# Reordering the loads and the preparation at the start of an attention and S4 convolution kernel

## The chip, the cores and the metric

The kernel runs on one core of one Trainium2 chip. The metric is the device time of one execution in microseconds (us). The engines: TensorE (PE, with its weight loads as PEld), VectorE (DVE), ScalarE (ACT), GpSimd (POOL), and SyncE (SP), which here only issues transfers; ACT and POOL issue some as well. SBUF is the on-chip memory, PSUM holds matmul results.

## What is computed

Two layers on separate inputs, each 2048 positions by 576 channels, whose outputs are put side by side:

```python
qkv = x @ wqkv                                # (2048,576) @ (576,1728), 32 heads of 18
scores = q k^T / sqrt(18), a key at most 255 positions back, softmax, @ v
a = that @ wo
# S4: one convolution kernel of 2048 taps for each channel
K[d,l] = Re sum_n C[d,n] * exp(dt[d]*A[d,n]*l) * dt[d]*B[d,n]        # n = 0..127, dt = exp(log_dt)
b = causal convolution of u with K (by FFT of length 4096) + u * Dskip
```

All inputs and outputs are float32, and the kernel keeps that accuracy with cheaper matmuls: an operand is scaled by a power of two and split into a high and a low float16 part (or into up to three bfloat16 parts).

## The kernel before

**Stages.** The program has a front (loads, scales, splits), then a loop up to about 423 us that runs three streams interleaved, then the transform of the convolution's taps, then the attention with the convolution beside it, and the output projection. Only the front and the way the loop begins are touched.

**The front of the projection** (`proj` up to its first yields, L184). To split x and wqkv it needs one power of two for each, from the largest magnitude of the whole array. `amax` (L163) takes the maximum of a block on DVE; `pow2_max` (L141) takes the maximum of those and reduces it over the 128 partitions on POOL; `pow2_of` (L149) turns it into the scale with four small DVE instructions. x is read for this as a flat block of 128 rows in four pieces and a rest, into the buffers that wh and wl will have later and into one of pool `pst`. Then wqkv comes in four column blocks of 432 by `load_rows` (L135), three transfers a block: rows 0 to 511 as four row groups of 128, and rows 512 to 575 twice, into both halves of the fifth group. So the fifth group holds its 64 rows doubled, and a matmul of 128 rows does their high and low parts in one. The weights' splits follow, per block wh on ACT (L215) and wl on DVE (L216).

**The front of the tables** (`s4_prep`, L274). It loads dt and A in two layouts, the multipliers c_ca, c_cm, c_cp and c_ct, and B and C, all from ACT's queue. It forms dt\*A (real and imaginary) over 96 partitions, three copies of 32, and `split3` (L261) splits each into three bfloat16 parts, one for each copy: `al` and `ps`, the stationary operands of the tables' matmuls (`outer`, L315). `wr` and `wi` are the products of B, C and dt.

**The loop's streams** are generators, and `merge` (L78) takes a step now of one and now of another, by the share that each has done. `proj`: for four chunks of 512 tokens, x comes in two halves, is split (L232 on ACT, L233 and L235 on DVE), and nine tiles of q and k and eight half tiles of v follow, 14 matmuls each (`mm14`, L166). A tile goes from PSUM by one ACT and one DVE instruction. Tiles and the u step share three PSUM buffers (pool `pps`). `tables`, for 36 groups of channels: exponents on ACT (mab, mg), phases by `fraction` (L324) on ACT and DVE, sines on ACT, `factors` on POOL (tr, t, A), `products` on POOL (m, L390), the Q table on DVE, and `taps` on PE (L428). `s1_u`: the first transform of u in 16 steps, 8 matmuls each.

**Order.** The order in which the program writes the instructions is not that of the engines in the front and the loop: a scheduler sets the order of each queue by its own estimates, with earlier written work first when several are ready. Inside `manual_schedule` the instructions keep the written order on each engine (the attention uses this already). In the profile before, instructions of that block stand on SP and DVE between ones written outside. Instructions on one engine run in the order of its queue, and one that waits holds those behind it.

## Time and profile before

| | |
|---|---|
| three runs | 1047.87, 1048.56, 1053.68 us; median 1048.56 |
| the profiled execution | 1042.13 us, span 1040.4 us, mean granted TensorE clock 0.968 |
| busy in the span | PE 81%, DVE 68%, ACT 55%, POOL 56% |
| moved from and to HBM | 88.60 MB read, 61.01 MB written |
| first projection matmul | 83.46 us |
| first product of the tables | 90.21 us |
| last tap | about 423 us |

Busy time of PE counts a matmul from its start to its modelled end, so a high share is not a peak rate. A group's line has the code line, engine, operation, output, inputs and shape; "idle before <-" names what ended the wait. In a table of stretches each engine's busy time is followed by its count of instructions.

### The profile page before, as it was taken

What the parts mean: (1) busy time and instruction counts of PE and PEld (TensorE: products, weight loads), DVE (VectorE), ACT (ScalarE), POOL (GpSimd) and SP (SyncE); (2) the same over time, 40 slices, a digit from 0 to 9 for tenths busy, and PEclk for the clock granted to TensorE, in tenths of its full rate; (3) what the DMA queues carried; (4) which work ended last, traced back from release to release, by engine and by line L of the source; (5) the groups of instructions that cost most, each with busy time, mean ns of one, the idle gap of its engine ahead of it and who ended that gap; (6) DMA issues with size and microseconds to landing.
All of it is one profiled execution on the core that took longest, in us unless ns stands there. A gap on an engine that the chain in (4) does not pass through costs nothing.

```text
span 1040.4 us, 26877 instructions
## 1 busy us (share of the span) xinstructions
PE 840.5 (81%) x10364; PEld 448.8 (43%) x10364; DVE 710.3 (68%) x1806; ACT 572.3 (55%) x895; POOL 585.5 (56%) x714
## 2 busy tenths in 40 slices
PE   0148997997989899677888888878887989988788
PEld 0024465565556457444343333323333444444345
DVE  2887567556565575655768888778877767678454
ACT  0486666665766666233565655645655555644461
POOL 0007768566576586200466676647775847766770
PEclk9998999999999899889899999989999999999999
DMA  9934444453543344564544465445634563579863
GB/s 272 286 93 119 99 111 120 111 127 88 128 110 91 75 95 92 158 198 128 160 125 143 136 184 176 116 124 160 202 104 143 169 183 99 141 193 240 232 180 124
DMA packets 151383, 151.74 MB, mean 146 GB/s; under 512 B 36808, under 2 KB 129224, under 8 KB 150552
## 3 DMA queue, kind: packets, MB, share of 16 engines
q1 hardware_dynamic: 143624, 131.45, 46.3%
q0 software_dynamic: 6128, 14.60, 5.1%
q10 hardware_dynamic: 1504, 3.99, 1.3%
q8 instruction: 81, 1.33, 0.6%
q14 instruction: 46, 0.38, 0.1%
HBM read 88.60 MB, written 61.01 MB: 144 GB/s over the span
## 4 chain that ended last, share of the span: by engine, by line
PE 41%; DVE 21%; DMA 13%; issue 9%; ACT 7%; POOL 4%; SPq 3%; DVEq 0%; ACTq 0%; POOLq 0%
PE pp L174 9%; PE r L648 5%; PE po L712 5%; PE r L918 4%; PE pp L472 3%; PE kp L428 3%; PE r L511 3%; PE r L519 3%; PE ST L689 3%; DVE jk L655 2%; PE x L320 2%; DMA c_ca<-in_c_ca_dram 2%; DVE qb L639 2%; DMA gk<-g 2%; DMA K<-in_wqkv_dram 2%
## 5 line engine op out<-in xcount | busy, mean ns | idle before, releaser
L655 DVE CUSTOM_DVE_ANT_0 jk<-r,bias 128x288 f32<-128x288 f32 (+7 forms) x512 | 199.8, 433 | 87.1 <-PE r L648 84.8
L700 POOL TENSOR_SCALAR_AFFINE_SELECT P<-P 128x512 f32<-128x512 f32 x240 | 167.7, 727 | 162.1 <-ACT P L691 159.6
L691 ACT ACTIVATE P<-ST,esc 128x1024 f32<-128x1024 f32 (+1 forms) x192 | 202.2, 1058 | 93.9 <-PE ST L689 93.3
L390 POOL TENSOR_TENSOR m<-A,tr 128x1024 f32<-128x1024 f32 x72 | 145.7, 2046 | 88.4 <-PE kp L428 88.4
L648 PE MATMUL r<-K,qb 128*64 128x288 f16 (+7 forms) x1024 | 130.1, 298 | 41.4 <-DVE t L542 11.5
L648 PEld LDWEIGHTS <-qb 128*64 128x64 f16 x1024 | 60.4, 110 | 124.5 <-issue 67.5
L712 PE MATMUL po<-P,V 128*32 128x256 f32 (+2 forms) x1408 | 100.6, 400 | 15.7 <-POOL P L700 6.1
L548 POOL TENSOR_TENSOR Y<-t,t 64x288 f32<-64x288 f32 x64 | 53.2, 831 | 75.9 <-DVE t L543 74.0
L472 PE MATMUL pp<-ut,w 128*128 128x288 f32 x128 | 44.3, 476 | 61.2 <-DMA ut<-in_u_dram 46.7
L428 PE MATMUL kp<-Q,m 128*32 128x64 f32 x4608 | 77.3, 220 | 7.8 <-issue 5.2
L428 PEld LDWEIGHTS kp<-Q,m 128*32 128x32 f32 x4608 | 67.8, 110 | 29.5 <-issue 23.3
L689 PE MATMUL ST<-Q,K 64*128 64x384 f16 (+2 forms) x704 | 74.0, 282 | 3.5 <-DMA Q<-mt 3.5
L130 ACT ACTIVATE g<-pp 128x288 f32<-128x288 f32 x96 | 36.9, 411 | 50.5 <-DMA gk<-g 24.9
L712 PEld LDWEIGHTS po<-P,V 128*32 128x32 f32 x1408 | 36.4, 111 | 50.3 <-issue 30.8
L472 PEld LDWEIGHTS pp<-ut,w 128*128 128x128 f32 x128 | 25.5, 215 | 74.1 <-issue 46.9
L549 POOL TENSOR_TENSOR Y<-t,t 64x288 f32<-64x288 f32 x64 | 53.9, 842 | 3.7
L174 PE MATMUL pp<-xh,wh 128*128 128x512 f16 x180 | 49.3, 392 | 6.8 <-DVE xh L235 5.2
L368 POOL TENSOR_TENSOR tr<-tr,mab 128x768 f32<-128x768 f32 x18 | 33.0, 1833 | 38.0 <-ACT tr L337 37.8
L331 DVE TENSOR_TENSOR k<-x,k 128x512 f32<-128x512 f32 (+1 forms) x54 | 34.0, 639 | 29.7 <-ACT k L330 29.2
L243 DVE SCALAR_TENSOR_TENSOR qst<-pp,qst 128x512 f16<-128x512 f32 x36 | 24.6, 684 | 42.8 <-ACT qst L242 29.1
L472 PE MATMUL pp<-K,w 128*128 128x288 f32 x128 | 44.0, 488 | 11.4 <-ACT g L130 10.0
L174 PEld LDWEIGHTS <-wh 128*128 128x128 f16 x324 | 31.8, 100 | 45.2 <-issue 11.9
(175 smaller groups left out, 1768.4 us busy)
## 6 DMA issues: line engine op xcount, KB each, us to landing
gx<-g SPq DMA_DIRECT2D x32, 288.0 KB
qd<-qst SPq DMA_DIRECT2D x72, 128.0 KB
gk<-g SPq DMA_DIRECT2D x32, 288.0 KB
tx<-gx SPq DMA_DIRECT2D x16, 576.0 KB
tk<-gk SPq DMA_DIRECT2D x16, 576.0 KB
h<-ho SPq DMA_DIRECT2D x16, 576.0 KB
Q<-qd SPq DMA_DIRECT2D x32, 216.0 KB
vd<-vst SPq DMA_DIRECT2D x16, 304.0 KB
```

The costliest lines, as they stand in the source:

```text
L174: self.nc.tensor.matmul(ps, u, v, start=(i == 0), stop=(i == len(ops) - 1))
L390: self.nc.gpsimd.tensor_tensor(m, A[:, ch, a0:a0 + 8].unsqueeze(3).to_broadcast(sh), tr[:, ch, part, 0:8].unsqueeze(2).to_broadcast(sh), o ...
L428: nc.tensor.matmul(kp[32 * st:32 * st + 32, c % 2 * JJ2 + j, :], m[:, ch, a0:a0 + 32], Q[:, ch, term % 2, :], start=(term == 0), stop=(ter ...
L472: nc.tensor.matmul(ps, self.w1[:, part, :], src[:, o:o + k], start=True, stop=True)
L548: nc.gpsimd.tensor_tensor(Y[par][0:64], t1[sl, 0], t2[sl, 0], op=OP.subtract)
L549: nc.gpsimd.tensor_tensor(Y[par][64:128], t1[sl, 1], t2[sl, 1], op=OP.add)
L648: nc.tensor.matmul(ps[64 * b:64 * b + 64, :n], self.qb[:, b, t, :], d["K"][:, b, k0:k0 + n], start=True, stop=True, skip_group_check=True)
L655: nc.vector.tensor_tensor_reduce(out=jk[:, :n], in0=ps[:, :n], in1=self.bias[:, 288 - n:], scale=1.0, scalar=-3e38, op0=OP.add, op1=OP.max ...
L689: nc.tensor.matmul(ps[:, u, o:o + n], d["K"][h, jp, k0:k0 + 128], d["Q"][h, jp, q0:q0 + n], start=True, stop=True, skip_group_check=True)
L691: nc.scalar.activation(pt[:, 2 * jp:2 * jp + 2, lo:hi], ps[:, :, lo:hi], AF.Exp, scale=self.esc)
L700: nc.gpsimd.affine_select(v, v, pattern=[[0, 4], [sg, 128]], compare_op=OP.is_ge, fill=0.0, base=-1 if far else 0, channel_multiplier=-sg)
L712: nc.tensor.matmul(self.po[32 * j:32 * j + 32, t0 * 128:t1 * 128], V[:, kb * 76 + 19 * j:kb * 76 + 19 * j + 32], pt[:, j, o:o + (t1 - t0) ...
```

## The change

The loads get a written order on SP: wqkv in four blocks, n_A_re, the first two halves of x (512 tokens), n_A_im, the other tokens of x as flat blocks in two buffers, dt, and the four parameters. The multipliers and one small input stay on ACT's queue. The host lays x and wqkv out so that a block is a single transfer with the doubled rows in it. The first two halves of x give part of the maximum and stay for the first split, so that these tokens are read once. Scales, splits and the tables' operands are written beside them in one function, `front`, whose order is fixed on each engine by `manual_schedule`. The three passes over ps (one product, two differences) move from DVE to POOL. The operand al gets its second and third parts from one residue in place; two ACT copies over 32 partitions each become one over 64. The weights' scale is formed ahead of that of x, by a reduction of its own. In the first merge stand one step for x, six projection tiles, 16 table steps and one u step, where four weight splits, 16 table steps and two u steps stood; the second merge has 49 projection steps in place of 56, and 15 u steps in place of 14. `load_rows`, `pow2_scale`, `split3` and `s4_prep` go.

```diff
+def columns(m, n):
+
+    r = m[np.r_[0:576, 512:576]].reshape(5, 128, -1, n)
+    return np.ascontiguousarray(r.transpose(1, 2, 0, 3))
+
+
...
+    def load_x(self, b):
+        t = self.p["raw"].tile([128, 5, 256], F32, name="raw")
+        self.nc.sync.dma_start(t, self.a["x"][:, b])
+        return t
+
+    def split_w(self, c, part):
+        cs = slice(c * 432, c * 432 + 432)
+        wh, wl = self.w
+        if part == 0:
+            self.nc.scalar.activation(wh[:, :, cs], self.wf[:, c], AF.Copy, scale=self.sw)
+        else:
+            self.nc.vector.scalar_tensor_tensor(wl[:, :, cs], self.wf[:, c], self.sw, wh[:, :, cs],
+                                                op0=OP.mult, op1=OP.subtract)
+
+    def split_x(self, raw):
+        nc = self.nc
+        xh = self.p["x"].tile([128, 5, 512], F16, name="xh")
+        xl = self.p["x"].tile([128, 4, 512], F16, name="xl")
+        for hf, t in enumerate(raw):
+            h = xh[:, :, hf * 256:hf * 256 + 256]
+            nc.scalar.activation(h, t, AF.Copy, scale=self.sx)
+            nc.vector.scalar_tensor_tensor(xl[:, :, hf * 256:hf * 256 + 256], t[:, 0:4], self.sx, h[:, 0:4],
+                                           op0=OP.mult, op1=OP.subtract)
+            nc.vector.scalar_tensor_tensor(h[64:128, 4], t[64:128, 4], self.sx[64:128], h[64:128, 4],
+                                           op0=OP.mult, op1=OP.subtract)
+        return xh, xl
+
+    def front(self):
+
+
+        nc, a, wp, sp, s4, tp = self.nc, self.a, self.p["wq"], self.p["const"], self.p["s4c"], self.p["prep"]
+        tt, pt, act = nc.vector.tensor_tensor, nc.gpsimd.tensor_tensor, nc.scalar.activation
+        self.mul, par, nA, flat = {}, {}, {}, []
+        dtn = tp.tile([96, NQ], F32, name="dtn")
+        dt = tp.tile([128, D], F32, name="dt")
+        for n in ("A_re", "A_im"):
+            nA[n] = tp.tile([96, NQ, 128], F32, name="n" + n)
+        nc.scalar.dma_start(dtn, a["ldtn"])
+        wf = self.wf = self.p["K"].tile([128, 4, 5, 432], F32, name="K")
         for c in range(4):
-            cs = slice(c * 432, c * 432 + 432)
-            self.load_rows(wr[:, :, cs], a["wqkv"], cs)
-            self.amax(amx[:, 5 + c:6 + c], wr[:, :, cs])
-        yield
-        px, self.sx = self.pow2_scale(amx[:, 0:5], "x")
-        pw, self.sw = self.pow2_scale(amx[:, 5:9], "w")
+            nc.sync.dma_start(wf[:, c], a["wqkv"][:, c])
+        for n in ("c_ca", "c_cm", "c_cp", "c_ct"):
+            self.mul[n] = s4.tile(list(a[n].shape), BF, name=n)
+            nc.scalar.dma_start(self.mul[n], a[n])
+        nc.sync.dma_start(nA["A_re"], a["n_A_re"])
+        raw = [self.load_x(hf) for hf in range(2)]
+        nc.sync.dma_start(nA["A_im"], a["n_A_im"])
+        cols = (0, 2304, 4608, 5760, 6912)
+        for c in range(4):
+            flat.append(tp.tile([128, 2304], F32, name="flat%d" % (c % 2))[:, :cols[c + 1] - cols[c]])
+            nc.sync.dma_start(flat[c], a["xf"][:, cols[c]:cols[c + 1]])
+        nc.sync.dma_start(dt, a["ldt"].partition_broadcast(128))
+        for n in S4_PARAMS:
+            par[n] = tp.tile([128, D], F32, name="in_" + n)
+            nc.sync.dma_start(par[n], a["p_" + n])
+        self.halfpi = s4.tile([128, 1], F32, name="halfpi")
+        nc.vector.memset(self.halfpi, math.pi / 2)
+        amx = sp.tile([128, 10], F32, name="amx")
+        wh = wp.tile([128, 5, 1728], F16, name="wh")
+        wl = wp.tile([128, 5, 1728], F16, name="wl")
+        self.w = wh, wl
+        self.vst = [wp.tile([128, 32, 19], F32, name="vst%d" % i) for i in range(2)]
+        for v in self.vst:
+            nc.gpsimd.memset(v, 1.0)
+        act(dtn, dtn, AF.Exp)
+        dtp = tp.tile([96, NQ], F32, name="dtp")
+        nc.vector.tensor_scalar(dtp, dtn, 1 / (2 * math.pi), None, op0=OP.mult)
+        wide = lambda z: z.unsqueeze(2).to_broadcast([96, NQ, 128])
+        al, ps = (s4.tile([96, NQ, 128], BF, name=n) for n in ("al", "ps"))
+        ra, rp = (tp.tile([64, NQ, 128], F32, name="res%d" % n) for n in range(2))
+        self.al, self.ps = al, ps
+        for c in range(4):
+            self.amax(amx[:, c:c + 1], wf[:, c])
+        wm, wg = self.pow2_max(amx[:, 0:4], "w")
+        tt(nA["A_re"], nA["A_re"], wide(dtn), op=OP.mult)
+        act(al, nA["A_re"], AF.Copy)
+        pw, self.sw = self.pow2_of(wg, "w")
+        self.split_w(0, 0)
+        for c in range(2):
+            self.amax(amx[:, 4 + c:5 + c], raw[c])
+        self.split_w(1, 0)
+        self.split_w(0, 1)
+        tt(ra, nA["A_re"][0:64], al[0:64], op=OP.subtract)
+        act(al[0:64], ra, AF.Copy)
+        pt(nA["A_im"], nA["A_im"], wide(dtp), op=OP.mult)
+        act(ps, nA["A_im"], AF.Copy)
+        pt(rp, nA["A_im"][0:64], ps[0:64], op=OP.subtract)
+        for c in range(2):
+            self.amax(amx[:, 6 + c:7 + c], flat[c])
+        self.split_w(2, 0)
+        tt(ra[32:64], ra[32:64], al[32:64], op=OP.subtract)
+        act(ps[0:64], rp, AF.Copy)
+        for c in range(2, 4):
+            self.amax(amx[:, 6 + c:7 + c], flat[c])
+        xm, xg = self.pow2_max(amx[:, 4:10], "x")
+        px, self.sx = self.pow2_of(xg, "x")
+        self.xs = self.split_x(raw)
+        act(al[32:64], ra[32:64], AF.Copy)
+        pt(rp[32:64], rp[32:64], ps[32:64], op=OP.subtract)
+        act(ps[32:64], rp[32:64], AF.Copy)
+        self.split_w(3, 0)
+        self.split_w(1, 1)
+        act(dt, dt, AF.Exp)
+        wr = self.wr = s4.tile([128, D], F32, name="wr")
+        wi = self.wi = s4.tile([128, D], F32, name="wi")
+        tt(par["B_re"], par["B_re"], dt, op=OP.mult)
+        tt(par["B_im"], par["B_im"], dt, op=OP.mult)
+        y1, y2 = (tp.tile([128, D], F32, name="x%d" % n) for n in range(2))
+        tt(y1, par["C_re"], par["B_re"], op=OP.mult)
+        tt(y2, par["C_im"], par["B_im"], op=OP.mult)
+        tt(wr, y1, y2, op=OP.subtract)
+        tt(par["C_re"], par["C_re"], par["B_im"], op=OP.mult)
+        tt(par["C_im"], par["C_im"], par["B_re"], op=OP.mult)
+        tt(wi, par["C_re"], par["C_im"], op=OP.add)
         pz = self.pz = sp.tile([128, 1], F32, name="pz")
         self.esc = sp.tile([128, 1], F32, name="esc")
         nc.vector.scalar_tensor_tensor(pz, px, 0.25, pw, op0=OP.mult, op1=OP.mult)
         nc.vector.scalar_tensor_tensor(self.esc, pz, 18.0 ** -0.5, pz, op0=OP.mult, op1=OP.mult)
-        wh = wp.tile([128, 5, 1728], F16, name="wh")
-        wl = wp.tile([128, 5, 1728], F16, name="wl")
-        for c in range(4):
-            cs = slice(c * 432, c * 432 + 432)
-            nc.scalar.activation(wh[:, :, cs], wr[:, :, cs], AF.Copy, scale=self.sw)
-            nc.vector.scalar_tensor_tensor(wl[:, :, cs], wr[:, :, cs], self.sw, wh[:, :, cs],
-                                           op0=OP.mult, op1=OP.subtract)
-            yield
+        self.split_w(2, 1)
+        self.split_w(3, 1)
+
...
+    def proj(self):
+        nc, a, dp = self.nc, self.a, self.p["dram"]
+        self.qd = dp.tile([64 * 54 + 18, L], F16, name="qd")
+        self.vd = dp.tile([8, 128, 16, 76], F32, name="vd")
+        (wh, wl), vst = self.w, self.vst
         self.K = self.p["K"].tile([128, 64, 144], F32, name="K")
-        vst = [wp.tile([128, 32, 19], F32, name="vst%d" % i) for i in range(2)]
-        for v in vst:
-            nc.gpsimd.memset(v, 1.0)
         S = 2.0 ** -24
         for c in range(4):
             cs = slice(c * 512, c * 512 + 512)
-            xh = self.p["x"].tile([128, 5, 512], F16, name="xh")
-            xl = self.p["x"].tile([128, 4, 512], F16, name="xl")
-            for hf in range(2):
-                t = self.p["raw"].tile([128, 5, 256], F32, name="raw")
-                self.load_rows(t, a["xT"], slice(c * 512 + hf * 256, c * 512 + hf * 256 + 256))
-                h = xh[:, :, hf * 256:hf * 256 + 256]
-                nc.scalar.activation(h, t, AF.Copy, scale=self.sx)
-                nc.vector.scalar_tensor_tensor(xl[:, :, hf * 256:hf * 256 + 256], t[:, 0:4], self.sx, h[:, 0:4],
-                                               op0=OP.mult, op1=OP.subtract)
-                nc.vector.scalar_tensor_tensor(h[64:128, 4], t[64:128, 4], self.sx[64:128], h[64:128, 4],
-                                               op0=OP.mult, op1=OP.subtract)
+            xh, xl = self.split_x([self.load_x(2 * c + hf) for hf in range(2)]) if c else self.xs
             yield
...
                 proj, tables, s1u = self.proj(), self.tables(), self.s1_u()
-                next(proj)
-                with ExitStack() as e2:
+                with ExitStack() as e2, self.tc.manual_schedule():
                     self.pool(e2, "prep", 1)
-                    self.s4_prep()
+                    self.front()
                 for n, b in (("ab", 2), ("abt", 1), ("mab", 4), ("mg", 4), ("fr", 2), ("Q", 2), ("P", 2)):
                     self.pool(e1, n, b)
-                merge((part(proj, 4), 4), (part(tables, 16), 16), (part(s1u, 2), 2))
-                merge((proj, 56), (tables, 308), (s1u, 14))
+                merge((part(proj, 7), 7), (part(tables, 16), 16), (part(s1u, 1), 1))
+                merge((proj, 49), (tables, 308), (s1u, 15))
                 for _ in part(s1k, 10):
                     pass
...
     arrays = {
-        "xT": np.ascontiguousarray(inputs["A_x"][0].T),
-        "wqkv": np.ascontiguousarray(inputs["A_wqkv"][:, np.r_[np.arange(1152).reshape(64, 18).T.ravel(), 1152:1728]]),
+        "x": columns(inputs["A_x"][0].T, 256),
+        "xf": np.ascontiguousarray(inputs["A_x"][0, 512:].reshape(128, -1)),
+        "wqkv": columns(inputs["A_wqkv"][:, np.r_[np.arange(1152).reshape(64, 18).T.ravel(), 1152:1728]], 432),
```

More of the change, by code (lines that the diff above doesn't have):

```diff
@@ L132, in evac @@
             self.nc.vector.tensor_copy(out, in_)
-    def load_rows(self, t, src, cols):
-        nc, n = self.nc, cols.stop - cols.start
-        nc.sync.dma_start(t[:, 0:4, :n], src[0:512, cols].rearrange("(k p) c -> p k c", p=128))
-        nc.sync.dma_start(t[0:64, 4, :n], src[512:576, cols])
-        nc.sync.dma_start(t[64:128, 4, :n], src[512:576, cols])
     def pow2_max(self, parts, nm):
@@ L158, in pow2_of @@
         return p, r
-    def pow2_scale(self, parts, nm):
-        return self.pow2_of(self.pow2_max(parts, nm)[1], nm)
     def amax(self, out, v):
@@ L182, in store_heads @@
         nc.sync.dma_start(stack(97, 32)[:, 2], st[32:64, 0])
-    def proj(self):
-        nc, a, wp, dp, sp = self.nc, self.a, self.p["wq"], self.p["dram"], self.p["const"]
-        self.qd = dp.tile([64 * 54 + 18, L], F16, name="qd")
-        self.vd = dp.tile([8, 128, 16, 76], F32, name="vd")
-        amx = sp.tile([128, 9], F32, name="amx")
-        wr = self.p["K"].tile([128, 5, 1728], F32, name="K")
-        flat = a["xT"].rearrange("r c -> (r c)").rearrange("(p n) -> p n", p=128)
-        for i, nm in enumerate(("wh", "wl")):
-            t = wp.tile([128, 4320], F32, name=nm)
-            for c in range(2):
-                o = 2160 * (2 * i + c)
-                nc.sync.dma_start(t[:, 2160 * c:2160 * c + 2160], flat[:, o:o + 2160])
-                self.amax(amx[:, 2 * i + c:2 * i + c + 1], t[:, 2160 * c:2160 * c + 2160])
-        t = self.p["pst"].tile([128, 576], F32, name="qst")
-        nc.sync.dma_start(t, flat[:, 8640:])
-        self.amax(amx[:, 4:5], t)
-        for c in range(4):
-            cs = slice(c * 432, c * 432 + 432)
-            self.load_rows(wr[:, :, cs], a["wqkv"], cs)
-            self.amax(amx[:, 5 + c:6 + c], wr[:, :, cs])
-        yield
-        px, self.sx = self.pow2_scale(amx[:, 0:5], "x")
-        pw, self.sw = self.pow2_scale(amx[:, 5:9], "w")
@@ L258, in proj @@
                 yield
-    def split3(self, src, name):
-        nc, tp = self.nc, self.p["prep"]
-        T = self.p["s4c"].tile([96, NQ, 128], BF, name=name)
-        r = tp.tile([96, NQ, 128], F32, name="res")
-        nc.scalar.activation(T, src, AF.Copy)
-        nc.vector.tensor_tensor(r, src, T, op=OP.subtract)
-        nc.scalar.activation(T[32:64], r[32:64], AF.Copy)
-        nc.scalar.activation(T[64:96], r[64:96], AF.Copy)
-        nc.vector.tensor_tensor(r[64:96], r[64:96], T[64:96], op=OP.subtract)
-        nc.scalar.activation(T[64:96], r[64:96], AF.Copy)
-        return T
```

40 lines of the change are left out of this document (removed).

## The prediction

> **What bounds the kernel now.** I read the page's slices first, to see where the engines stand still, then the windows of the stage that the change touches. In the slices each digit is a fortieth of the span (26 us), busy tenths.
>
> ```profile
> PE   0148997997989899677888888878887989988788
> DMA  9934444453543344564544465445634563579863
> ```
>
> PE does almost nothing in the first two slices and 4 tenths in the third; DMA is full just there. From slice four on PE is at 8 or 9 until the attention. So the start is a stage of its own, bound by loads and by what follows them.
>
> ```profile
> 2.00:46.00 44.00, 0.00 (x0) 0.00 (x0) 23.45 (x11) 9.38 (x7) 1.22 (x3) 1.00 1.03 309
> 46.00:83.00 37.00, 17.70 (x39) 8.93 (x40) 31.61 (x36) 29.79 (x35) 1.47 (x2) 0.95 0.39 106
> 90.00:423.00 333.00, 301.52 (x5770) 188.21 (x5768) 214.56 (x309) 212.00 (x378) 228.13 (x182) 0.98 0.45 104
> ```
>
> Columns: stretch, PE, PEld, DVE, ACT, POOL busy, clock, DMA share, GB/s. Up to 46 us the loads run at 309 GB/s and full share, while DVE is half idle. From 46 to 83 the loads are over, but DVE (85%) and ACT (81%) do the preparation: the second limit. From 90 to 423 PE is busy 91%, the table and projection loop. The timeline names the steps.
>
> ```profile
> 6.23 2.40 DVE L164 TENSOR_REDUCE amx<-wh 128x1 f32<-128x2160 f32 x1 [5.30 <-DMA wh<-in_xT_dram]
> ...
> 44.94 4.70 DVE L164 TENSOR_REDUCE amx<-K 128x1 f32<-128x2160 f32 x2
> 58.08 0.15 DVE L145 TENSOR_REDUCE xm<-amx 128x1 f32<-128x5 f32 x1
> 61.28 0.15 DVE L157 TENSOR_SCALAR xr<-xr 128x1 f32<-128x1 f32 x1
> 61.80 4.08 ACT L215 ACTIVATE wh<-K,wr 128x2160 f16<-128x2160 f32 x2
> 70.05 0.85 ACT L337 ACTIVATE mab<-x 128x384 f32<-128x384 f32 x2
> 81.02 0.97 ACT L330 ACTIVATE k<-x 128x384 int32<-128x384 f32 x2
> 82.35 1.15 DVE L331 TENSOR_TENSOR k<-x,k 128x384 f32<-128x384 f32 x2
> 83.46 0.63 PE L174 MATMUL pp<-xh,wh 128*128 128x512 f16 x1
> 90.21 3.87 POOL L390 TENSOR_TENSOR m<-A,tr 128x1024 f32<-128x1024 f32 x2
> ```
>
> The last maximum of wqkv is known at 49.6, yet both scales wait until 58 behind table operands on DVE. The eight weight splits and the splits of x all lie behind 61.8. The projection starts at 83.5 and the tables' products at 90.2. The change moves these two points; what it is worth is how far both move, and how much of that the loop to 423 keeps.
>
> **The change, part by part.** Prices, min/median/max ns where three stand:
>
> ```profile
> L164 DVE TENSOR_REDUCE amx<-K x4: 2392/2394/2402, 35.4 to 47.3; 128x1 f32<-128x2160 f32 x4
> L298 DVE TENSOR_TENSOR nA_re<-nA_re,dtn x1: 2545/2545/2545, 31.0 to 31.0; 96x2304 f32<-96x2304 f32 x1
> L216 DVE SCALAR_TENSOR_TENSOR wl<-K,wr,wh x4: 2462/2467/2469, 64.4 to 74.6; 128x2160 f16<-128x2160 f32 x4
> L215 ACT ACTIVATE wh<-K,wr x4: 2081/2094/2143, 61.8 to 72.4; 128x2160 f16<-128x2160 f32 x4
> L232 ACT ACTIVATE xh<-raw,xr x8: 1347/1356/1427, 75.3 to 333.5; 128x1280 f16<-128x1280 f32 x8
> L233 DVE SCALAR_TENSOR_TENSOR xl<-raw,xr,xh x8: 1276/1730/3012, 77.0 to 338.5; 128x1024 f16<-128x1024 f32 x8
> L235 DVE SCALAR_TENSOR_TENSOR xh<-raw,xr,xh x8: 484/486/2079, 78.3 to 343.7; 64x256 f16<-64x256 f32 x8
> L310 DVE TENSOR_TENSOR wr<-x,x x1: 748/748/748, 57.4 to 57.4; 128x576 f32<-128x576 f32 x1
> 42.41 2.12 ACT L269 ACTIVATE al<-res 32x2304 bf16<-32x2304 f32 x1
> 28.97 0.67 ACT L296 ACTIVATE dt<-dt 128x576 f32<-128x576 f32 x1
> L390 POOL TENSOR_TENSOR m<-A,tr x72: 1947/1954/2940, 90.2 to 416.1; 128x1024 f32<-128x1024 f32 x72
> L368 POOL TENSOR_TENSOR tr<-tr,mab x18: 1807/1824/1942, 85.3 to 398.7; 128x768 f32<-128x768 f32 x18
> ```
>
> *Bytes.* The old order brings x once flat (4.72 MB) and wqkv (4.42 MB) and later loads x's first 512 tokens again. The new one brings wqkv 4.42, x's two halves 1.31, the flat rest 3.54: 0.1 MB more, because of the doubled rows. The front's total stays 13.4 MB. I gain nothing on the rate: 309 GB/s, although rows are longer. Fewer transfers on SP (one instead of three per block) I cost at nothing: SP was not what DVE waited for.
>
> *When x is known.* Ahead of the second flat block's end lie w1 0.13, wqkv 4.42, multipliers 0.74 (beside them on ACT's queue), n_A 1.77, x 1.31 and flat 2.36, together 10.7 MB: 34.7 us, landed at about 37. Meanwhile DVE does four maxima of wqkv (9.6), n_A_re (2.5), two maxima of raw (1280 columns at 1.11 ns: 2.8), one wl (2.5) and a residue (2.5), 20 us, the last perhaps held by POOL to 37. The flat blocks have two buffers: blocks 2 and 3 are issued only when the maxima (2.56 each) of 0 and 1 are done, about 40 and 42.6. SP holds the parameters behind that wait, and nothing else of the front; they are due at 59.7. A small load costs its bytes plus some 1.8 us (the first row above: 1.1 MB from 0.8 to 6.2, 3.6 at the rate), so block 3 lands at 46.3 and its maximum (1.28) ends near 47.6. The reduction over partitions and the four small steps took 58.08 to 61.4 among other work; alone I take 2.2. The scale of x stands at about 50, instead of 61.4; that of w, with it the splits of blocks 0 to 2 on ACT, is long out of the way.
>
> *From there to PE.* xh twice on ACT, 2.7: 52.7. DVE's xl and doubled rows, 2 x (1.28+0.49) = 3.5, but POOL's third pass over ps runs then. That pass has 2304 columns; the two POOL rows give 1.9 to 2.4 ns a column, 4.4 to 5.5 us. The timeline shows what such a pass does to DVE:
>
> ```profile
> 245.47 4.85 POOL L390 TENSOR_TENSOR m<-A,tr 128x1024 f32<-128x1024 f32 x2 [0.43 <-PE kp L428]
> ...
> 246.33 2.17 DVE L233 SCALAR_TENSOR_TENSOR xl<-raw,xr,xh 128x1024 f16<-128x1024 f32 x1 [2.04 <-ACT xh L232]
> ```
>
> xl took 2.17 instead of 1.28, so the lower bound for this meeting is 0 and the upper a whole pass, 5.5; I take 2.5. DVE is through x at 56; the first projection tile starts near 54.5, 29 us before 83.5.
>
> *The rest of the front.* ACT after xh: al, ps, wh block 3, Exp of dt: 3 x 2.1 + 0.7, to 59.7. DVE: wl block 1 (2.5, 58.5), then eight products of parameters (8 x 0.75 = 6.0) that wait for that Exp, 65.7, wl blocks 2 and 3 (4.9): 70.6. Evacuations of projection tiles need DVE too, and three PSUM buffers hold only three tiles; if none slips in between, PE stands from 64 to 70. That is priced below.
>
> *The tables.* Before, mab at 70.05 led to products at 90.2, of which about 5 were wh, xh and their like on ACT. After, mab can run at 59.7, but the fractions (82.35 before) need DVE, free at 70.6. From there 90.2 - 82.35 = 7.9 remain: products at 78.5, **12 us earlier**.
>
> *What PE has done by then.* Rows for the projection and for u's first stage up to 90.2, and the pace of one projection tile and of one u step in the chain of waits:
>
> ```profile
> 0.00:90.20 90.20, 6.03 (x21) 2.47 (x22) 0.96 0.71 205
> ...
> 0.00:90.20 90.20, 13.38 (x24) 7.25 (x24) 0.96 0.71 205
> ...
> 183.99 3.02 PE pp L174 x14
> ...
> 323.89 2.14 PE pp L472 x8
> ```
>
> 21 matmuls are 1.5 tiles, 24 are three u steps. The new first merge runs six tiles beside the same 16 table steps, but one u step. So PE is ahead by 4.5 x 3.02 - 2 x 2.14 = 9.3 us of work. The bounds for its worth are 0 (the loop waits for tables) and 9.3 (it waits for PE).
>
> ```profile
> POOL m L390 <- PE kp L428: 85.5, 14, 11.2
> ```
>
> This wait, the loop's largest, says that POOL stands behind PE's order more than the reverse; yet 9% of PE's time is gaps. I take about half, 5.
>
> *Sum.* 12 + 5 = 17 us off the profiled execution, 1042.1 us (span 1040.4 and 1.7 around it): 1025. The runs' median is 1048.56, 6.4 above it, so 1031.5. A check from PE alone: 29 us earlier, less what it had done by then (three u steps, 6.4, and the tables' first matmuls, some 3 by my estimate) and less the 6 us stall, is 13 or 14. Stages after 423 stay as they are and move as a block.
>
> **The rule that speaks against it.** The Trainium skill, "SBUF — State Buffer", section "Who interferes with whom", says that GpSimd and a VectorE instruction with two SBUF inputs take turns on a shared port pair, and whichever comes second waits for the whole instruction. The 2.17 us above agrees in kind. The three new passes on POOL, 13 to 16 us by the rows, would by it push DVE back by as much where no wait hides it.
>
> **The rivals.** *Hidden (0 to 5 us gained).* The passes of POOL (13 to 16 us) meet wl, the residues and xl on DVE, one each. Then DVE ends its front at 70 + 8 to 12, products come at 86 to 90, and the early tiles stall on three PSUM buffers, so the lead is lost: 1043.5 to 1048.5. For it: the maximum of 3012 ns for xl. Against: two of the meetings fall where DVE waits for loads anyway. The page named above would make this the likelier case.
>
> *All of it (27 and more).* Other instructions slip into DVE's gaps at 50 to 65, three tiles are evacuated there, the tables' fractions too, and PE's lead closes some of its 30 us of gaps: 29 us, 1020.
>
> *Slower.* POOL's passes subtract a bf16 operand over 96 and 64 partitions, for which no row exists. With T for a pass, n_A_im landed at 30: two passes and a copy end at 32 + 2T, and the reduction over partitions stands behind them on POOL, so x's scale is at 34 + 2T; ps is whole at 36 + 3T, products 10 later. From T = 15 (6.5 ns a column, against 2.4 and at worst 2.9 in the rows) it is later than 90.2. At T = 18 the loss is 10 us: 1058.
>
> **How the numbers follow.** The forecast case has 0.60 with a range of its own, gains of 8 to 26: 1022 to 1040. All of it 0.13, hidden 0.18, slower 0.09. The range for 8 in 10 goes from 1017 to 1046, which cuts off slower, the worst end of hidden and a few hundredths below. Half a per cent is 5.2 us, about what can be told from no change here. Faster takes the first two and a sixth of hidden: 0.76; same 0.15; slower 0.09.
>
> **What would show it.** Right: the first projection matmul (83.46) at 52 to 57; products (90.21) at 75 to 81; PE busy between 54 and 64; x's scale near 50; the last tap near 406. Wrong: POOL's passes over 8 us, the scale of x after 58, DVE busy with front work after 75, the last flat block landing after 50, or products early and the last tap still near 420: the lead and the shift were then given back to another wait in the loop.

## The result, and the profile after

| | before | changed |
|---|---|---|
| median of the runs | 1048.21 us (4 runs, 1045.96 to 1053.68) | 1034.36 us (4 runs, 1033.64 to 1035.59) |
| ratio, 95% interval | 1 | 0.9861 [0.9822, 0.9901] |
| the profiled execution | 1042.13 us, span 1040.4, clock 0.968 | 1033.93 us, span 1032.2, clock 0.970 |
| first projection matmul | 83.5 | 60.1 |
| first product of the tables | 90.2 | 94.4 |
| last tap | 423.3 | 417.0 |

The kernel is faster by 1.4%, 13.9 us by the medians and 8.2 between the two profiled executions. The forecast was 1031.5. The time came out 2.9 us above it, but the two terms of its sum came out otherwise: the projection moved 23 us forward, the products moved 4 us back. Part of the difference by the medians may go with the clock: in the experiments' runs of the kernel before, those that were granted less than 0.96 take 1046.0 us on average (26 runs, without one slow run of 1084.81 us at 0.826), the others 1043.0 (13 runs), and all ten runs of the changed kernel were granted 0.969 to 0.974. The two profiled executions, at 0.968 and 0.970, compare like with like; whether the change itself raises the clock is not shown.

First the slices and the same stretches as before.

```profile
PE   0079979989997989677888888778888989988787
DMA  9645544535452532654534476345634563478863
```

```profile
2.00:46.00 44.00, 0.00 (x0) 0.00 (x0) 33.54 (x18) 13.92 (x9) 10.18 (x6) 1.00 0.82 278
46.00:83.00 37.00, 24.71 (x87) 10.95 (x88) 24.46 (x30) 18.05 (x22) 6.26 (x2) 0.95 0.47 129
90.00:423.00 333.00, 301.18 (x5747) 190.66 (x5745) 217.33 (x314) 215.10 (x388) 232.23 (x187) 0.97 0.45 106
```

PE's third slice went from 4 to 7 tenths, the fourth from 8 to 9. DVE's work moved ahead of 46 us (33.5 us where 23.5 stood), and from 46 to 83 PE has 24.7 us where it had 17.7. The mean of the loads up to 46 fell, 278 GB/s where 309 stood, but not because they were slower. Up to 30 us they were faster (340 GB/s, before 302); then they stood still, with 0 GB/s from 34 to 39 us. Changed, then before:

```profile
2.00:30.00 28.00, 0.00 (x0) 0.00 (x0) 17.57 (x14) 7.49 (x5) 3.45 (x5) 1.00 1.00 340
```

```profile
2.00:30.00 28.00, 0.00 (x0) 0.00 (x0) 9.61 (x4) 2.07 (x3) 1.22 (x3) 1.00 1.01 302
```

The stretch from 90 to 423 is as full as before: the loop itself did not change.

The timeline of the front in extracts, sorted here by engine, many rows left out (start, duration, engine, line, operation; in brackets the idle time before it and what ended that):

```profile
39.41 0.35 SPq L231 DMA_DIRECT2D flat<-in_xf_dram  x1
41.87 0.35 SPq L231 DMA_DIRECT2D flat<-in_xf_dram  x1
...
28.15 4.04 POOL L265 TENSOR_TENSOR nA_im<-nA_im,dtp 96x2304 f32<-96x2304 f32 x1 [7.37 <-DMA nA_im<-in_n_A_im_dram]
41.22 4.54 POOL L267 TENSOR_TENSOR res<-nA_im,ps 64x2304 f32<-64x2304 f32 x1 [9.04 <-ACT ps L266]
52.49 0.38 POOL L146 PARTITION_ALL_REDUCE xg<-xm  x1 [6.73 <-issue]
59.69 5.88 POOL L279 TENSOR_TENSOR res<-res,ps 32x2304 f32<-32x2304 f32 x1 [6.81 <-issue]
...
28.16 6.30 DVE L192 SCALAR_TENSOR_TENSOR wl<-K,wr,wh 128x2160 f16<-128x2160 f32 x1 [0.75 <-ACT wh L190]
41.87 6.30 DVE L271 TENSOR_TENSOR res<-res,al 32x2304 f32<-32x2304 f32 x1
53.48 0.15 DVE L157 TENSOR_SCALAR xr<-xr 128x1 f32<-128x1 f32 x1
70.44 0.76 DVE L286 TENSOR_TENSOR in_B_re<-in_B_re,dt 128x576 f32<-128x576 f32 x1 [8.92 <-ACT dt L283]
77.26 4.84 DVE L192 SCALAR_TENSOR_TENSOR wl<-K,wr,wh 128x2160 f16<-128x2160 f32 x2
85.89 0.56 DVE L352 TENSOR_TENSOR k<-x,k 128x384 f32<-128x384 f32 x1 [2.58 <-ACT k L351]
...
65.60 2.12 ACT L280 ACTIVATE ps<-res 32x2304 bf16<-32x2304 f32 x1 [6.13 <-POOL res L279]
69.75 0.67 ACT L283 ACTIVATE dt<-dt 128x576 f32<-128x576 f32 x1
...
58.48 0.82 PE L341 MATMUL x<-c_ca,al 96*128 96x384 bf16 x2 [3.52 <-ACT al L278]
60.06 2.34 PE L171 MATMUL pp<-xh,wh 128*128 128x512 f16 x5
69.82 1.03 PE L171 MATMUL pp<-xl,wh 128*128 128x512 f16 x4
73.86 2.29 PE L171 MATMUL pp<-xh,wh 128*128 128x512 f16 x5 [3.02 <-DVE qst L318]
```

Three readings. *DVE and POOL hold each other.* A split wl lasts 6.30 us beside a pass on POOL (28.16 against 28.15) where another takes 2.4 (4.84 for two), and a residue 6.30 beside the next pass (41.87 against 41.22). *One late pass holds a chain.* POOL's third pass starts at 59.7 and ends at 65.6. ACT stands for it 6.13 us with a copy of ps at the head of its queue, behind which wh's last block and the Exp of dt stand, and DVE stands 8.92 us for that Exp. *PE has three tiles.* From 60.06 to 70.8 it runs three without a gap, then it waits 3.02 us for an evacuation (the ACT and DVE instructions that empty a tile's PSUM buffer).

The taps, as a group of one line, give the end of the loop: before and changed.

```profile
L428 PE MATMUL kp<-Q,m x4608: 216/219/244, 92.8 to 423.3; 128*32 128x64 f32 x192
```

```profile
L449 PE MATMUL kp<-Q,m x4608: 216/219/317, 99.9 to 417.0; 128*32 128x64 f32 x192
```

The first starts 7.1 us later and the last 6.3 earlier: the loop after it is 13 us shorter, as it would be if projection work that stood in it was done ahead of it; the experiments test this.

### The profile page after: what moved, and what is told of

Its sections match the earlier page's. It is cut to its first block, busy times and chain, and to the rows that moved or that the text cites. A ratio compares the mean times of both kernels' runs of the same rounds, so it can differ in the third digit from the quotient of the medians.

```text
span 1032.2 us, 26840 instructions
## 1 busy us (share of the span) xinstructions
PE 839.1 (81%) x10364; PEld 448.3 (43%) x10364; DVE 711.4 (69%) x1805; ACT 567.6 (55%) x893; POOL 598.3 (58%) x717
## 4 chain that ended last, share of the span: by engine, by line
PE 43%; DVE 20%; DMA 11%; issue 10%; ACT 8%; POOL 5%; SPq 2%; DVEq 0%; ACTq 0%; POOLq 0%
PE pp L171 9%; PE r L669 5%; PE po L733 5%; PE kp L449 4%; PE r L939 4%; PE pp L493 4%; PE r L532 3%; PE ST L710 3%; PE r L540 3%; DVE jk L676 2%; PE x L341 2%; DMA gk<-g 2%; POOL P L721 2%; ACT P L712 2%; DMA nA_re<-in_n_A_re_dram 1%
## 5 line engine op out<-in xcount | busy, mean ns | idle before, releaser
L493 PE MATMUL pp<-ut,w 128*128 128x288 f32 x128 | 42.0, 450 | 65.0 <-DMA ut<-in_u_dram 51.7
L449 PE MATMUL kp<-Q,m 128*32 128x64 f32 x4608 | 81.9, 224 | 8.2 <-DVE Q L432 5.1
L449 PEld LDWEIGHTS kp<-Q,m 128*32 128x32 f32 x4608 | 71.1, 113 | 34.4 <-issue 24.1
L493 PEld LDWEIGHTS pp<-ut,w 128*128 128x128 f32 x128 | 23.3, 199 | 78.3 <-issue 52.0
L389 POOL TENSOR_TENSOR tr<-tr,mab 128x768 f32<-128x768 f32 x18 | 33.2, 1843 | 39.5 <-ACT tr L358 39.5
L353 DVE TENSOR_SCALAR ab<-k 128x512 int32<-128x512 int32 (+1 forms) x54 | 52.6, 986 | 0.4
```

What stands on the lines that cost most here:

```text
L449: nc.tensor.matmul(kp[32 * st:32 * st + 32, c % 2 * JJ2 + j, :], m[:, ch, a0:a0 + 32], Q[:, ch, term % 2, :], start=(term == 0), stop=(ter ...
L493: nc.tensor.matmul(ps, self.w1[:, part, :], src[:, o:o + k], start=True, stop=True)
```

## The experiments

Two theories were tested. *PE*: the end follows the projection work that PE has done when the loop begins. *T*: the end follows the start of the tables' products. Each ratio is against runs of the kernel before on the same chip. The numbers of all runs stand in one table behind the first four.

**The old shares of the streams on the new front.**

```diff
-                merge((part(proj, 7), 7), (part(tables, 16), 16), (part(s1u, 1), 1))
-                merge((proj, 49), (tables, 308), (s1u, 15))
+                merge((part(tables, 16), 16), (part(s1u, 2), 2))
+                merge((proj, 56), (tables, 308), (s1u, 14))
```

> The changed kernel with the merge shares of before: no projection step beside the first 16 table steps, two u steps there, then 56 projection, 308 table and 14 u steps. The front is that of the changed kernel. Reference: 1034.4 us for the changed kernel, 1048.2 before. Theory PE (the end follows the projection work that PE has done by the time the tables run, 6 tiles of 3.02 us less a u step of 2.14, and the start of the products counts only through PE's gaps): that lead is lost, 8 to 12 us slower than the changed kernel, 1042 to 1046. Theory T (the end follows the start of the tables' products, at 94.4 us now): 0 to 3 us slower, or a little faster if the products start earlier because DVE and PSUM are free for them.

Measured: 1041.46 us, ratio 0.9968 [0.9948, 0.9989]. The products come 3 us earlier than in the changed kernel, and the gain falls from 1.4% to 0.3%, 11 us by the ratios: T's 0 to 3 us fails, PE's 8 to 12 fits. Its timeline shows what PE does instead.

```profile
71.01 4.13 PE L493 MATMUL pp<-ut,w 128*128 128x288 f32 x10 [7.62 <-ACT g L136]
74.97 1.24 PE L171 MATMUL pp<-xh,wh 128*128 128x512 f16 x5
```

No tile stands in the first merge, but a second step of u does, and PE stands 7.6 us with that step ahead of the tiles. The evacuation g that it needs is on ACT behind the copy of ps that waits for POOL. The first tile comes at 75.0. The edit takes the early tiles away and puts the second step of u ahead; it does not tell the two apart.

**The third pass over ps back on DVE.**

```diff
-        pt(rp[32:64], rp[32:64], ps[32:64], op=OP.subtract)
+        tt(rp[32:64], rp[32:64], ps[32:64], op=OP.subtract)
```

> Only the third pass over ps goes back from POOL to DVE. It started on POOL at 59.7, 6.8 us after the reduction over partitions had ended, and ran 5.9 us, with ACT waiting behind it to 65.6 and DVE to 70.4 for Exp of dt. On DVE it takes 2.55 us and can run at about 59 to 61, so ACT goes on at about 61.5: Exp of dt at 65.5 in place of 69.8, products near 90 in place of 94.4. If the POOL gap of 6.8 us is only a pause that nothing waits for, products stay at 94. Theory T: 4 us faster than 1034.4, 1030. Theory PE: the stall of PE at 71 to 74 goes, 1 to 3 us faster.

Measured: 1031.39 us, 0.9875 [0.9847, 0.9903]; products at 89.9, 4.5 us earlier. By the ratios it can't be told from the changed kernel, so it decides nothing between T and PE.

**In addition Exp of dt and wh's last block ahead of the copies of al and ps on ACT.**

```diff
-        act(al[32:64], ra[32:64], AF.Copy)
-        pt(rp[32:64], rp[32:64], ps[32:64], op=OP.subtract)
-        act(ps[32:64], rp[32:64], AF.Copy)
         self.split_w(3, 0)
-        self.split_w(1, 1)
         act(dt, dt, AF.Exp)
+        self.split_w(1, 1)
+        act(al[32:64], ra[32:64], AF.Copy)
+        tt(rp[32:64], rp[32:64], ps[32:64], op=OP.subtract)
+        act(ps[32:64], rp[32:64], AF.Copy)
```

> As the one with the third pass on DVE, and on ACT wh block 3 and Exp of dt stand ahead of the copies into al and ps. DVE gets its eight products from about 61 in place of 70.4, its front ends near 72 in place of 82, products of the tables start at 82 to 85 in place of 94.4; the first projection tile stays at 60. Theory T: 9 to 12 us faster than the changed kernel, 1023 to 1025. Theory PE: only the stall of 3 us and some gaps go, 2 to 5 us faster, 1029 to 1032.

Measured: 1027.97 us, 0.9846 [0.982, 0.9872]. Products came at 90.8, not earlier than in the run above, so what T needed for its test did not happen. DVE's front did end earlier, at 77.3. But the first tile on PE moved back, behind a matmul of the tables that needs al, and the first phases of the tables (on ps) stand behind tiles until 82.3.

```profile
61.25 0.82 PE L341 MATMUL x<-c_ca,al 96*128 96x384 bf16 x2 [5.78 <-ACT al L281]
61.87 1.17 PE L493 MATMUL pp<-ut,w 128*128 128x288 f32 x2
62.83 2.34 PE L171 MATMUL pp<-xh,wh 128*128 128x512 f16 x5
...
82.31 0.33 PE L341 MATMUL x<-c_ca,ps 96*128 96x384 bf16 x1
```

From 62.8 PE runs without a stall, and the tables' matmuls stand among its tiles. Whether this order is worth anything at all the intervals leave open.

**No fixed order.**

```diff
-                with ExitStack() as e2, self.tc.manual_schedule():
+                with ExitStack() as e2:
```

> The same front without the fixed order: the scheduler sets the order of each engine's queue by its own estimates, loads included. If the written order carries the gain, this gives part of it back: 3 to 10 us slower than 1034.4, with the first projection tile later than 60 or the wait on POOL elsewhere. If the new layout and the early maxima of wqkv carry it, it is within 3 us.

Measured: 1031.92 us, 0.988 [0.9852, 0.9908]: as the changed kernel. The scheduler's own order of the same instructions has the scale of x 5 us later, at 58.6, and yet the first tile at 61.5: PE is through with the first matmuls on al and u's step at 58.5, and the tile waits for xh alone. So the gain does not need the fixed order. How much of it the host's layout, the order in which the program writes the loads and the new parts carry, each alone, is not tested.

All runs in one table. PE's column is its busy time from 0 to 100 us, from the windows of each profiled execution.

| kernel | first tile | first product | PE busy to 100 | last tap | median | ratio |
|---|---|---|---|---|---|---|
| before, six tiles early | 77.4 | 102.6 | 30.5 | 431.2 | 1053.38 | 1.0064 |
| before | 83.5 | 90.2 | 33.2 | 423.3 | 1048.21 | 1 |
| old shares | 75.0 | 91.3 | 33.3 | 423.8 | 1041.46 | 0.9968 |
| three tiles early | 60.1 | 92.6 | 36.6 | 412.9 | 1033.90 | 0.9911 |
| changed | 60.1 | 94.4 | 40.0 | 417.0 | 1034.36 | 0.9861 |
| changed, again | 60.1 | 94.5 | 39.3 | 415.5 | 1034.01 | 0.9877 |
| nine tiles early | 60.3 | 101.6 | 40.5 | 415.6 | 1031.65 | 0.9892 |
| Exp and wh ahead on ACT | 62.8 | 90.8 | 40.3 | 410.9 | 1027.97 | 0.9846 |
| no fixed order | 61.5 | 90.1 | 41.6 | 413.2 | 1031.92 | 0.9880 |
| third pass on DVE | 60.4 | 89.9 | 42.9 | 413.5 | 1031.39 | 0.9875 |
| all passes on DVE | 55.0 | 88.2 | 47.7 | 407.5 | 1028.26 | 0.9818 |
| scale of x early | 52.1 | 84.7 | 49.6 | 407.3 | 1025.35 | 0.9793 |
| the same, u's step freed | 50.7 | 83.6 | 51.0 | 404.2 | 1023.67 | 0.9805 |
| u's step freed, nine tiles | 51.0 | 88.7 | 51.3 | 398.8 | 1019.29 | 0.9769 |

**The changed kernel again**, beside the next three on their chip.

> The changed kernel itself, beside the others of this group: a ratio to the kernel before of 0.982 to 0.990, the interval already seen, and the measure for the other three.

Measured: 1034.01 us, 0.9877 [0.9856, 0.9897].

**The scale of x earlier.** Four flat buffers, so no load waits for a maximum; the maxima of x stand ahead of residues and splits on DVE; the second and third pass over ps go back to DVE.

```diff
-            flat.append(tp.tile([128, 2304], F32, name="flat%d" % (c % 2))[:, :cols[c + 1] - cols[c]])
+            flat.append(tp.tile([128, cols[c + 1] - cols[c]], F32, name="flat%d" % c))
...
+        self.split_w(0, 1)
         px, self.sx = self.pow2_of(xg, "x")
         self.xs = self.split_x(raw)
-        act(al[32:64], ra[32:64], AF.Copy)
-        pt(rp[32:64], rp[32:64], ps[32:64], op=OP.subtract)
-        act(ps[32:64], rp[32:64], AF.Copy)
+        act(dt, dt, AF.Exp)
         self.split_w(3, 0)
         self.split_w(1, 1)
-        act(dt, dt, AF.Exp)
...
```

> The changed kernel with the scale of x and the parts of al earlier: four flat blocks in four buffers, so SP waits for none; on DVE the residues of al and the maxima of flat run in turn and wl block 0 comes only beside the reduction of x over partitions; passes two and three over ps go to DVE behind the split of x; Exp of dt goes right behind xh on ACT. The scale of x should stand near 42 to 44 in place of 53.5, the first projection tile near 46 to 48 in place of 60. Theory PE: the end follows PE's start, 8 to 14 us faster than the changed kernel (ratio to before near 0.975). Theory T: it follows the products, which can come some 6 to 12 us earlier than 94.4; both give a gain here. A third, that the loop is bound elsewhere once PE is ahead: less than 3 us.

Measured: 1025.35 us, 0.9793 [0.9766, 0.982], 8.7 us below the changed kernel beside it. The first tile comes 8 us earlier, as theory PE has it; the products come 10 us earlier, so T forecast a gain too. The scale stands at 45.3 and the tile at 52.1, both later than expected. POOL's reduction lasted 2.48 us where it took 0.38 in the changed kernel: a wl had begun on DVE 0.2 us ahead of it, and it ended 0.24 us after that. What holds the tile until 52.1 is u's step again:

```profile
41.98 2.46 DVE L192 SCALAR_TENSOR_TENSOR wl<-K,wr,wh 128x2160 f16<-128x2160 f32 x1
42.20 2.48 POOL L146 PARTITION_ALL_REDUCE xg<-xm  x1 [7.84 <-DVE xm L145]
...
45.29 0.15 DVE L157 TENSOR_SCALAR xr<-xr 128x1 f32<-128x1 f32 x1
...
48.57 2.08 ACT L190 ACTIVATE wh<-K,wr 128x2160 f16<-128x2160 f32 x1
...
50.99 1.32 PE L492 MATMUL pp<-ut,w 128*128 128x288 f32 x2 [4.78 <-ACT g L136]
```

**The kernel before with six tiles early.**

```diff
-                merge((part(proj, 4), 4), (part(tables, 16), 16), (part(s1u, 2), 2))
-                merge((proj, 56), (tables, 308), (s1u, 14))
+                merge((part(proj, 11), 11), (part(tables, 16), 16), (part(s1u, 1), 1))
+                merge((proj, 49), (tables, 308), (s1u, 15))
```

> The kernel before with the new merge shares alone: behind its four weight splits, one x step and six projection tiles beside the first 16 table steps, one u step in place of two, then 49, 308 and 15. Its front is untouched, its scales still come at 61 and x's split at 84. If the lead alone is the gain whatever the front, it is 8 to 11 us faster than before. Theory PE: PE has no work before 83 here, so six early tiles only push the tables back by as much: within 3 us of before, or slower.

Measured: 1053.38 us, 1.0064 [1.0046, 1.0083]: slower. On the old front the tiles find no free time of PE; products go to 102.6, and PE has done less by 100 us than without them (30.5 against 33.2). The shares pay only with the earlier scales, and the earlier scales hardly without the shares.

**The three passes on DVE.**

```diff
-        tt, pt, act = nc.vector.tensor_tensor, nc.gpsimd.tensor_tensor, nc.scalar.activation
+        tt, pt, act = nc.vector.tensor_tensor, nc.vector.tensor_tensor, nc.scalar.activation
```

> The changed kernel with all three passes over ps on DVE in the places that they have, and nothing on POOL but the two reductions. DVE gets 2.5 us three times; what it loses is the waits behind POOL: wl block 0 and the second residue of al took 6.30 each in place of 2.47 and 2.55. If the two engines hold each other for a whole instruction, wl and the residue go back to 2.5 and the scale of x comes 1 to 4 us earlier than 53.5 although DVE does more; products near 90, as the 6.8 us pause of POOL is gone too; 1 to 5 us faster than the changed kernel. If POOL's work was free, the scale of x comes 5 us later and the kernel is 3 to 5 us slower.

Measured: 1028.26 us, 0.9818 [0.9794, 0.9841], against 0.9877 for the changed kernel beside it, and the intervals do not meet: to have the passes on POOL cost 5.8 us. Its timeline and its first 100 us (PE, PEld, DVE, ACT, POOL, clock, DMA share, GB/s), with those of the changed kernel behind:

```profile
28.23 2.47 DVE L192 SCALAR_TENSOR_TENSOR wl<-K,wr,wh 128x2160 f16<-128x2160 f32 x1 [0.75 <-ACT wh L190]
...
33.09 2.54 DVE L265 TENSOR_TENSOR nA_im<-nA_im,dtp 96x2304 f32<-96x2304 f32 x1
...
45.33 2.55 DVE L271 TENSOR_TENSOR res<-res,al 32x2304 f32<-32x2304 f32 x1
...
52.20 0.15 DVE L157 TENSOR_SCALAR xr<-xr 128x1 f32<-128x1 f32 x1
```

```profile
0.00:100.00 100.00, 47.69 (x430) 23.11 (x431) 74.10 (x78) 48.77 (x62) 19.29 (x24) 1.00 0.68 200
```

```profile
0.00:100.00 100.00, 40.03 (x159) 18.02 (x162) 68.56 (x64) 44.82 (x54) 27.65 (x21) 0.98 0.63 190
```

wl takes 2.47 again and the residue 2.55. The pass that lasted 4.04 us on POOL takes 2.54 on DVE, which is less than the 3.8 that it cost the wl beside it. PE has 7.7 us more done by 100. The scale of x comes only 1.3 us earlier and the first tile 5.0: in this run u's first step is done on PE by 44.2, and the matmuls on al stand behind the tile's first four. So the 5.8 us are those of the whole edit, with the pause of POOL (last section) and the other order on PE in it, and not of the holding alone.

**Three and nine tiles early on the changed kernel.** The count in the first merge is 4 or 10 steps in place of 7 (one is x), the second merge has the rest.

```diff
-                merge((part(proj, 7), 7), (part(tables, 16), 16), (part(s1u, 1), 1))
-                merge((proj, 49), (tables, 308), (s1u, 15))
+                merge((part(proj, 4), 4), (part(tables, 16), 16), (part(s1u, 1), 1))
+                merge((proj, 52), (tables, 308), (s1u, 15))
```

> Changed kernel with three projection tiles in the first merge in place of six; the one step of u there stays, the other three tiles go to the second merge. Theory PE (the end follows the projection work that PE has behind it when the loop begins): three tiles are 9 us, so the end comes 5 to 10 us later than in the changed kernel, near the run with all the old shares (1041): 1039 to 1044, although products start earlier, near 88 to 91. Theory T (the end follows the start of the products): products 3 to 6 us earlier than 94.4 and the end as much earlier, 1028 to 1031. If neither: within 2 us of the changed kernel, and the second u step of the old shares was what cost 8 us.

> Changed kernel with nine projection tiles in the first merge in place of six. Theory PE: PE is already busy from 60 to the start of the products but for a stall of 3 us, so three more tiles find at most 3 us of free time and push the tables' matmuls and products back by 6 to 9 us (to 100 to 103); what PE gains in lead the tables lose: between 3 us faster and 6 us slower than the changed kernel, 1031 to 1040. Theory T: 6 to 9 us slower, 1040 to 1043. If the lead were worth its full 9 us whatever the tables do: 1025.

Measured: 1033.90 us, 0.9911 [0.9878, 0.9944], for three; 1031.65, 0.9892 [0.9859, 0.9925], for nine. Neither can be told from the changed kernel. So the count of early tiles, which was my reading of theory PE after the old shares (1039 to 1044 was expected for three), is not it. What the old shares lacked is rather a first tile at 60: they have none early, and the second u step with its wait ahead. Three tiles hold what PE does before its first stall, and here they suffice. Which of the two costs the old shares their gain was not tested alone. Products at 101.6 cost nothing by the ratio either: T fails a second time, and from the other side.

The waits from 90 to 425, first rows, changed and with three tiles (total, times, longest), show that the loop takes this differently:

```profile
POOL m L411 <- PE kp L449: 76.6, 15, 11.3
POOL tr L389 <- ACT tr L358: 39.5, 11, 23.8
```

```profile
POOL m L411 <- PE kp L449: 66.5, 14, 10.6
```

POOL waits 10 us less for PE with three tiles, and PE is busier in the loop: 299.5 us of the stretch 100 to 425 where the changed kernel has 293.5. Why the order of that run fills the loop better, and why its ratio shows nothing of it, is open.

**The early scale, with u's step freed.** On the version with the scale at 45:

```diff
-        pt(nA["A_im"], nA["A_im"], wide(dtp), op=OP.mult)
+        tt(nA["A_im"], nA["A_im"], wide(dtp), op=OP.mult)
...
-        self.split_w(3, 0)
         self.split_w(1, 1)
         tt(rp, nA["A_im"][0:64], ps[0:64], op=OP.subtract)
         act(ps[0:64], rp, AF.Copy)
+        self.split_w(3, 0)
```

> The version with the scale of x at 45 (four flat buffers), and in it the split of the fourth weight block behind the first residue of ps on ACT, so that the evacuation of u's step does not wait behind it with the first projection tile behind that on PE; the product over ps goes to DVE too, so no pass stays on POOL. Theory PE: first tile at 49 to 50.5 in place of 52.1, the end 1.5 to 3 us earlier than that version, 1022 to 1024.5. Rival: the product on DVE (2.5 us) stands ahead of the maxima of the flat blocks and delays the scale by as much, no gain: 1025 to 1028.

Measured: 1023.67 us, 0.9805 [0.977, 0.9839]; first tile at 50.7. No pass over ps is left on POOL. By the ratio not to be told from the version that it starts from.

**The early scale with nine tiles.** The shares of the nine on the version with u's step freed. (The expectation takes its numbers from the one before that, with the tile at 52.1.)

> The version with the scale of x at 45 (four flat buffers) with nine projection tiles in the first merge in place of six. Theory PE: from the first tile at 52.1 nine tiles are 27 us, to about 80, still ahead of the products at 84.7, but the tables' matmuls share that time: between 4 us faster and 3 us slower than that version, 1021 to 1028. Theory T: products 6 to 9 us later and the end as much, 1031 to 1034.

Measured: 1019.29 us, 0.9769 [0.9736, 0.9801], the fastest: 2.3% below the kernel before, and below the changed kernel's interval. Against the same version with six tiles the products come 5.2 us later (88.7, 83.6) and the last tap 5.4 earlier (398.8, 404.2): T fails a third time. The intervals of the two overlap, so the share of the three further tiles is not established. PE has done the same by 100 us in both (51.3, 51.0), so that does not tell them apart either.

*What the table says together.* Sorted by PE's busy time up to 100 us, the last tap falls from 431 to 399, 1.2 us by a straight line for each us that PE has done; single rows lie off that line by up to 6.5 us (three tiles early). Sorted by the first product the order is loose (94.4 ends earlier than 90.2, 101.6 earlier than 91.3). The time of the first tile sorts the rows nearly as well as PE's busy time, and the two go together. PE's busy time was looked at only after the runs, so this form of theory PE is what fits, and none of the runs varies it alone.

## Why the prediction was right, and where its steps were wrong

**The scale of x: 50 forecast, 53.5 measured.** The loads were faster than the 309 GB/s that were taken (340 up to 30 us), but that gained nothing: SP could issue flat blocks 2 and 3 only at 39.4 and 41.9 (about 40 and 42.6 were said), held by their two buffers. The window from 30 to 40 shows it:

```profile
30.00:40.00 10.00, 0.00 (x0) 0.00 (x0) 10.00 (x4) 3.10 (x3) 2.19 (x1) 1.00 0.33 129
```

DMA is at a third of its time while DVE is busy all 10 us, among them a wl and a maximum. The last maximum ended at 50.8, 3.2 us later than the 47.6 of the forecast: ahead of it on DVE stood the residue at 41.87, held by POOL (6.30 in place of 2.5). From there to the scale 2.7 us were needed where 2.2 were taken, with 1.5 in which POOL was not yet ready for the reduction (last section).

**The first tile: 54.5 forecast, 60.1 measured.** 3.5 us came with the scale. The other 2.1 are PE's queue, which the forecast did not look at: matmuls on al and u's last two stand ahead of the tile, the first of them waits until 58.48 for a copy that stands behind xh on ACT. The bracketed wait on al in the timeline above is that step.

**Products: 12 us earlier forecast, 4.2 later measured.** This is the step that failed. It let ACT run al, ps, wh and Exp in a row to 59.7 and did not ask what ps waits for. The copy of ps waits for POOL's third pass, which started at 59.69 and not beside the split of x, near 54. Its inputs stood at 47.9; it waited behind the reduction over partitions and a pause of 6.81 us (last section). The Exp ended at 70.4 instead of 59.7, DVE's front at 82.1 instead of 70.6: 11.5 us. The fractions then began at 85.89, 3.8 us after DVE was free, since their input k came late from ACT. From there to the products 8.6 us were needed where 7.9 were taken. 11.5 + 3.8 + 0.7 is the 16 us between 78.5 and 94.4. With the third pass alone on DVE the Exp started at 65.8 in place of 69.8 and the products came at 89.9, which bears this out for that pass. The forecast priced the passes on POOL as locks on DVE and not as waits for ACT, with ACT's queue behind them. A smaller slip: its own steps (52.7, the last xl and its rows 1.8, the hold 2.5) put the end of x on DVE at 57, not 56. It also counted each us of earlier products as one of the end, which the three failures of T do not bear out.

**The lock: 2.5 us forecast once, for xl.** xl was untouched (1.28). wl and the residue paid 3.8 each. The Trainium skill, "SBUF — State Buffer", section "Who interferes with whom", says that whichever starts second is blocked for the whole instruction; here wl lasted POOL's whole pass (4.04) and its own 2.3 after it, and with the passes on DVE it took 2.47: the traces agree. DVE's third meeting did not happen, since DVE stood for the Exp then, and POOL's pass that started behind wl took 5.88.

**PE's lead: 5 us forecast, out of 0 to 9.3.** It was mis-sized. With products 4 us later, the earlier projection carried the whole gain, 13.9 us by the medians and 8.2 in the profiled executions. The check from PE alone in the forecast (29 us earlier, less u's steps, the tables' matmuls and a stall) is the reckoning that comes nearest: with the tile at 60.1 in place of 54.5 and the stall at 3.0 in place of 6, its 13 to 14 become 83.5 - 60.1 - 6.4 - 3 - 3 = 11, between the two measures. Read directly, PE has 6.8 us more done by 100 (40.0 against 33.2), and the last tap is 6.3 us earlier. The count of tiles behind the 9.3 is not what sets the lead, as three tiles did as well. So it is luck that the sum came right: one term that was too small made up for one of the wrong sign.

**The rivals.** *Hidden* had the mechanism half right: DVE's front ended at 82 and products came later than even it said, by POOL's passes. Its conclusion failed, that the early tiles would stall and the lead be lost: three ran before the stall, and the stall was 3 us. *Slower* needed passes of 15 us; they took 4.04, 4.54 and 5.88. *All of it* at 1020 was not reached by the change; the fastest experiment reaches it, with the scale of x 7 us earlier, nine early tiles and none of the passes on POOL.

## What to carry to other kernels

Where a pipeline of several streams starts behind a long front, ask first which engine bounds the loop and how much of its own work it can do before the loop's other inputs are ready; an earlier start of another stream's inputs was worth little here, and a later one cost little. For each instruction moved to another engine, follow the queue of the engine that waits for it: one 6 us pass on POOL held ACT's copy, behind it the Exp, behind that eight instructions on DVE. Moving work from a busy engine to an idle one does not unload it when the two hold each other up: three passes of 2.5 us were cheaper on the busy one.

## What the runs showed of the hardware that was not expected

POOL pauses when it changes between the reduction over partitions and ordinary tensor instructions. In the changed kernel the reduction started 6.73 us after the pass before it had ended, though its input stood at 51.0, 1.5 us earlier; the pass after it started 6.81 us after the reduction, though its inputs stood at 47.9. At each of these changes POOL's queue holds instructions named MODIFY_POOL_CONFIG, right behind the work before the pause (the reduction's last at 46.0, the pass's at 52.8 and 52.9):

```profile
L146 POOLq MODIFY_POOL_CONFIG  x4: 4/20/37, 3.4 to 46.0; - x4
```

```profile
L279 POOLq MODIFY_POOL_CONFIG  x2: 83/83/83, 52.8 to 52.9; - x2
```

Without a fixed order the same change of kind took 6.05 us:

```profile
56.03 0.38 POOL L146 PARTITION_ALL_REDUCE xg<-xm  x1 [6.05 <-issue]
```

With all passes on DVE, there is no change between the two reductions, and the second began 0.1 us after its input was whole:

```profile
50.98 0.16 DVE L145 TENSOR_REDUCE xm<-amx 128x1 f32<-128x6 f32 x1
...
51.24 0.35 POOL L146 PARTITION_ALL_REDUCE xg<-xm  x1 [30.08 <-DVE xm L145]
```

The Trainium skill, "GPSIMD Engine Reference", section "Instruction dispatch", gives about 6 us, with no visible instruction, for the first call of newly loaded code on this engine; the pauses here agree with it in size. That they come again when the kind changes back, in both directions, the runs above show. In the kernel before, those instructions stand at 59.8, so the pause fell into 25 us in which POOL had nothing to do.
